# Stage 1 of a long convolution in row halves, its last quarter in two halves, the expert index spread in two row tiles, and a new order of issue

## The chip, the cores and the metric

One NeuronCore of a Trainium2 chip runs the kernel. The metric is the device time of one execution in microseconds (us), median of the runs. Engines are named as the profile names them: PE (TensorE; PEld its weight loads), DVE (VectorE), ACT (ScalarE), POOL (GpSimd), SP (SyncE, which issues nearly all DMAs).

## What is computed

Input u is [1, 2048, 512]; both halves run on the layer norm of what comes in, and each adds its result to it.

```python
# first half: a long convolution per channel (state space model, N = 128 modes)
dt = exp(log_dt); A = -exp(log_A_real) + 1j * A_imag; C = (C_real + 1j * C_imag) * dt[:, None]
P  = exp((A * dt[:, None])[:, :, None] * pos)               # 512 x 128 x 2048
K  = 2.0 * einsum("dn,dnl->dl", C, P).real                  # one filter of 2048 per channel
y  = irfft(rfft(u, 4096) * rfft(K, 4096), 4096)[:2048] + u * D_skip
# second half: 32 heads, each picks one of 16 x 16 experts
q  = einsum("nd,dhc->nhc", x, w_q); s1 = q[..., :128] @ k1.T; s2 = q[..., 128:] @ k2.T
e  = argmax(s1) * 16 + argmax(s2)                           # K = 1, so the softmax weight is 1
out = sum_h gelu(x . u[e_h]) * v[e_h]
```

## The kernel before

**Layout.** The 512 channels are worked in four quarters of 128 (c = 0 to 3). A position is l = 64 * l1 + s, with l1 of 32 and s of 64. The transform of 4096 points is done in two matmul stages, in f32, where each matmul of the code is two MATMUL instructions, each with its own LDWEIGHTS.

- *Filters* (`factors`, `tables`, `kgen`): for each of 32 table pieces i (8 to a quarter) GpSimd writes phases `pg` (L557) and magnitudes `mg` (L588, L594), ScalarE takes sine and cosine (L644 to L647), VectorE multiplies (`mg`, `gf`, L651 to L664), and a `kps` call (L690, 64 instructions on four column tiles of 32) sums over the modes. Two pieces fill one filter tile `k`, four tiles to a quarter (kt = 0 to 3).
- *Stage 1* (`stage1`, L471; `u_s1` for the signal, `k_s1` for the filter): for each tile kt two jobs of 8 matmuls. The weights are 128 x 64 (4 channels x 32 l1 in the rows, 64 values of s), the moving table `c1_s` has 128 columns (32 frequencies x 4 channels, block diagonal in the channels), real and imaginary part on two column tiles. ScalarE copies each job to `yu` or `yk` (L474).
- *Stage 2* (`stage2`, L488): 8 jobs a quarter, each 4 matmuls with full weights `c2_s` and 128 moving columns (the channels). For the signal ScalarE copies the result to `U`; for the filter (`k_s2`) VectorE multiplies it by `U` (L732, L733, L735). In the last quarter GpSimd does a third of the product (L743), out of a copy made by ScalarE (L739).
- *Inverse, first part* (`k_ia`, L764): 8 jobs a quarter, 16 instructions each, over the products. They wait for all 8 products of the quarter. ScalarE (in quarter 3 ScalarE and VectorE, L777) copies to `T`; quarters 0 to 2 go to DRAM (`t_d`), quarter 3 stays.
- *Weights of the second half* (`w_piece`): 32 pieces fold w_q with the keys (`wps`, L828), turn them (L836) and store them to DRAM (`w_d`). They are fillers; their last loads `w_q`, their high part (ScalarE) and low part `w_lo` (VectorE, L925) come at the start of the second half.
- *Second half*: 8 blocks of 256 positions. `inverse` (`ib`, L1036, then `h`, L1043), `center` and `variance` (layer norm), `scores` (`sc`, `xu`, L1150 and L1157; `index`, L1199 and L1202, gives the expert of each of 32 heads in `ix`), `select`: `ix` is transposed to `ixT` [32 heads, 256] (L1242), spread by matmuls `bc` (L1258, weights `sel` 32 x 128, one for each group of four heads) over the partitions, copied to `idxb` (L1262), compared with expert codes (`oh`, L1280), counted (`cnt`, L1290), multiplied with the gelu values, and `o` (L1327) applies v.

**Order.** Nothing is scheduled at run time. Every step is an entry of `Plan.add` (engine, a planner's price in us, the function, what it reads and writes, which PSUM buffers it takes and gives back), and a table of numbers, `ORDER`, says in which order the entries issue. Each engine executes its instructions in that order, as does SP's queue of DMAs. PSUM has seven buffers `psA` in the first half, and two `psC` and four `psD` in the second.

Of the kernel before, what the change touches and what calls it, by code (L numbers as in the profile page):

```python
# [1448 lines left out]
```

## Time and profile before

| | us |
|---|---|
| median of 3 runs | 505.17 (503.89 to 506.71) |
| profiled execution, its own time | 504.94 |
| its span, first to last instruction | 503.2 |

| engine | busy us | share of the span |
|---|---|---|
| PE | 449.0 | 89% |
| PEld | 390.3 | 78% |
| DVE | 407.8 | 81% |
| POOL | 325.5 | 65% |
| ACT | 298.3 | 59% |

The chain that ended last lies 50% on PE, 22% on DVE, and 10% each on ACT and POOL. The shares are means over the span: the table is read together with stretches of the program, as an engine can be full in one and idle in the next. The granted clock of TensorE was 0.986 of full over the run.

### The profile page before, as it was taken

The page shows a single profiled execution, that of the slowest core. Times are in us where ns is not written, and L with a number is a line of the kernel's source. Part 1 is how long each engine was busy: PE and PEld are TensorE (multiplying, and loading weights), DVE is VectorE, ACT ScalarE, POOL GpSimd, SP SyncE. Part 2 cuts the span into 40 slices and gives each one's busy share as a digit, 9 for nine tenths or more (in the row PEclk, how much of TensorE's full clock was granted, in tenths as well). Part 3 has the DMA queues.
Part 4 walks back from the last instruction along what each step waited for, and adds up shares of the span by engine and source line. Part 5 has one row for each costly group of instructions (what it writes and reads, how often), then busy time and mean ns, then how long its engine had stood idle before and what let it go on. Part 6 is the DMA issues. An engine that isn't in the chain of part 4 may idle for free.

```text
span 503.2 us, 16702 instructions
## 1 busy us (share of the span) xinstructions
PE 449.0 (89%) x7206; PEld 390.3 (78%) x7206; DVE 407.8 (81%) x708; ACT 298.3 (59%) x594; POOL 325.5 (65%) x344
## 2 busy tenths in 40 slices
PE   0266879999998999999998889999999999999985
PEld 0144568888997999889997787877878888787874
DVE  5998998899968998899745574888979686978984
ACT  4867799967987588967965362644043430416230
POOL 4989989999999999997824303572163516536130
PEclk9998799999999999999999899999999999999999
DMA  8959474234033300631017689310171311010012
GB/s 253 403 198 381 143 288 148 66 86 179 2 111 124 85 3 1 212 126 45 1 61 259 200 275 283 127 61 1 57 227 55 109 63 43 1 44 0 1 68 62
DMA packets 27362, 61.05 MB, mean 121 GB/s; under 512 B 7028, under 2 KB 14456, under 8 KB 26136
## 3 DMA queue, kind: packets, MB, share of 16 engines
q1 hardware_dynamic: 27136, 59.85, 34.9%
q8 instruction: 57, 0.93, 0.7%
q10 hardware_dynamic: 152, 0.13, 0.1%
q14 instruction: 17, 0.14, 0.1%
HBM read 46.08 MB, written 13.89 MB: 119 GB/s over the span
## 4 chain that ended last, share of the span: by engine, by line
PE 50%; DVE 22%; ACT 10%; POOL 10%; issue 4%; DMA 3%; SPq 1%; ACTq 0%; DVEq 0%; POOLq 0%
PE sc L1150 12%; PE ia L764 9%; DVE oh L1280 5%; PE s2yk L488 3%; PE xu L1157 3%; PE kps L690 3%; PE s2yu L488 3%; POOL pg L557 3%; PE s1u L471 3%; DVE st L232 2%; PE o L1327 2%; PE ib L1036 2%; PE cnt L1290 2%; ACT t L645 2%; POOL mg L594 2%
## 5 line engine op out<-in xcount | busy, mean ns | idle before, releaser
L557 POOL TENSOR_TENSOR pg<-PS 128x1024 int32<-128x1024 int32 x32 | 68.8, 2150 | 0.5
L588 POOL TENSOR_TENSOR mg<-TS 128x1024 f32<-128x1024 f32 x32 | 62.6, 1958 | 7.2 <-PE kps L690 4.5
L1280 DVE TENSOR_SCALAR oh<-idxb,ec_s 128x2048 bf16<-128x2048 bf16 (+1 forms) x72 | 50.3, 757 | 6.8 <-ACT idxb L1262 6.8
L764 PE MATMUL ia<-ca_s,U 128*128 128x128 f32 x256 | 50.6, 280 | 0.4 <-POOL U L743 0.4
L1060 POOL TENSOR_TENSOR vs<-hc 128x256 f32<-128x256 f32 x8 | 7.0, 872 | 62.6 <-ACT hc L1083 62.6
L1192 POOL TENSOR_TENSOR ks<-kq 128x512 f32<-128x512 bf16 x16 | 17.2, 1078 | 45.9 <-DVE kq L1186 44.8
L645 ACT ACTIVATE t<-t,halfpi 128x512 f32<-128x512 f32 x64 | 42.4, 662 | 2.1
L1150 PE MATMUL sc<-w_hi,hhi 128*128 128x480 f32 x128 | 42.4, 412 | 0.0
L644 ACT ACTIVATE t<-pg 128x512 f32<-128x512 int32 x64 | 38.9, 609 | 3.2 <-DVE gf L652 2.2
L764 PEld LDWEIGHTS ia<-ca_s,U 128*128 128x128 f32 x256 | 39.8, 196 | 0.6 <-POOL U L743 0.6
L647 ACT ACTIVATE t<-pg 128x512 f32<-128x512 int32 x64 | 38.2, 608 | 2.8 <-POOL pg L557 1.5
L764 PE MATMUL ia<-ca_s,yk 128*128 128x128 f32 x192 | 38.1, 280 | 0.4 <-DVE mg L664 0.4
L1150 PE MATMUL sc<-w_lo,hhi 128*128 128x480 f32 x128 | 38.4, 380 | 0.0
L1150 PE MATMUL sc<-w_hi,hlo 128*128 128x480 f32 x128 | 38.3, 380 | 0.0
L594 POOL TENSOR_TENSOR mg<-TS 128x512 f32<-128x512 f32 x32 | 37.4, 1170 | 0.4
L690 PE MATMUL kps<-mg 128*32 128x64 f32 x1024 | 34.0, 230 | 3.8 <-DVE mg L664 2.2
L488 PE MATMUL s2yk<-yk,c_s 128*128 128x128 f32 x256 | 34.7, 282 | 1.1 <-ACT yk L474 0.7
L471 PE MATMUL s1u<-c_s,xs 128*64 128x128 f32 x512 | 33.3, 277 | 2.5 <-DVE xs L508 1.6
L690 PE MATMUL kps<-gf 128*32 128x64 f32 x1024 | 33.7, 229 | 1.8 <-issue 1.8
L488 PEld LDWEIGHTS s2yk<-yk,c_s 128*128 128x128 f32 x256 | 30.6, 191 | 4.2 <-issue 1.4
L488 PE MATMUL s2yu<-yu,c_s 128*128 128x128 f32 x256 | 32.6, 279 | 0.3
L471 PEld LDWEIGHTS s1u<-c_s,xs 128*64 128x64 f32 x512 | 27.6, 137 | 5.4 <-DVE xs L508 1.7
(198 smaller groups left out, 1377.5 us busy)
## 6 DMA issues: line engine op xcount, KB each, us to landing
wq<-wq SPq DMA_DIRECT2D x25, 512.0 KB, 4.5
t_d<-T SPq DMA_DIRECT2D x24, 256.0 KB, 3.4
Tb<-t_d SPq DMA_DIRECT2D x8, 768.0 KB, 6.0
x<-xa SPq DMA_DIRECT2D x8, 512.0 KB, 5.6
xs<-xb SPq DMA_DIRECT2D x16, 256.0 KB, 5.3
xt<-xt SPq DMA_DIRECT2D x8, 512.0 KB, 4.8
out<-ob SPq DMA_DIRECT2D x7, 512.0 KB, 3.0
c_s<-wq SPq DMA_DIRECT2D x4, 512.0 KB, 8.3
```

What stands on the lines that cost most here:

```text
L471: T.matmul(ps[64 * k:64 * k + 64, g, :], lhs8(4 * n + g), c1_s[:, k], start=True, stop=True)
L488: T.matmul(ps[:, k, :], c2_s[:, kk, :], y[:, :, kk, :], start=True, stop=True)
L557: G.tensor_tensor(view(pg, 0, [[32, 2 * NC], [8, 4], [1, 8]]), view(t["PS"], 1024 + off, [[1, 2 * NC], [128, 4], [0, 8]]), view(t["PS"], 8 ...
L588: G.tensor_tensor(view(mg, 0, [[96, NC], [8, 8], [1, 8]]), view(ts, 512 + 8 * o, [[8, NC], [1, 8], [0, 8]]), view(ts, 8 * o, [[8, NC], [0, ...
L594: G.tensor_tensor(view(mg, 64, [[96, NC], [8, 4], [1, 8]]), view(ts, 1536 + o, [[1, NC], [64, 4], [0, 8]]), view(ts, 1024 + 8 * o, [[8, NC ...
L644: A.activation(p, pg[:, :, k], AF.Abs)
L645: A.activation(p, p, AF.Sin, scale=-SINSCALE, bias=halfpi)
L647: A.activation(p, pg[:, :, k], AF.Sin, scale=SINSCALE)
L690: T.matmul(kps[32 * q:32 * q + 32, 2 * g + h, :], m[:, d, 64:96], m[:, d, 0:64], start=(e == 0), stop=(e == 1))
L764: T.matmul(ps[:, g, :], t[:, 4 * n + g].rearrange("p a b -> p (a b)"), ca_s[:, s, :], start=(s == 0), stop=(s == 1))
L1150: T.matmul(ps[:, 512 * h:512 * h + 480], t[x_][:, q, ts], I[w_][:, q, 480 * h:480 * h + 480], start=(q == 0 and x_ == w_), stop=(q == 3 an ...
L1280: V.tensor_scalar(oh[:, :, 0:ln], t["idxb"][:, :, sl], S["ec"][:, 4 * e + j:4 * e + j + 1], None, op0=ALU.is_equal)
```

## The change

1. *Stage 1 in row halves* (`stage1_rows`, for u and k in quarters 2 and 3: 16 pairs of jobs). A matmul takes the upper or the lower 64 rows, which hold two of the four channels, and so 64 columns of the table (`c1_s` gets a third part of 64 columns for this). Row half h and part k give four quarters of the array; the halves write two PSUM buffers, taken together. A pair of jobs before is 32 instructions of 128 x 64 weights and 128 moving columns; now it is 64 instructions of 64 x 64 weights and 64 moving columns.
2. *Quarter 3 in halves* (`SEGS`): stage 2 of the filter, the products and `k_ia` work on 64 channels at a time. A `k_s2` job covers 8 frequencies and 64 channels in place of 4 and 128, and so has 16 instructions in place of 8. The first four `k_ia` jobs depend on the first four products, the others on the last four.
3. *Index spread in two row tiles* (`index`, `select`, `sel`): `ix` holds the 32 indices twice, `ixT` has 64 rows, `sel` is loaded twice, and a `bc` job issues the matmuls of two groups of heads in turn, on rows 0 to 31 and 32 to 63, into two `psD` buffers.
4. *A new table ORDER* of 1712 entries in place of 1728; the first 232 are as before.

```diff
+    SEGS = (1, 1, 1, 2)
...
+    HALF = dict(u=(2, 3,), k=(2, 3,))
+
+    def stage1_rows(dst, lhs8, kt, nm, r, tiles, key):
+        job, k = {}, None
+        for n in range(2):
+            def mm(n=n, job=job):
+                if n == 0:
+                    for h in range(2):
+                        bank(job, f"{nm}_{h}", h)
+                for g in range(4 * n, 4 * n + 4):
+                    for k in range(2):
+                        for h in range(2):
+                            hs = slice(64 * h, 64 * h + 64)
+                            T.matmul(flat(job[h], 64)[64 * k:64 * k + 64, g], lhs8(g)[hs], c1_s[hs, k, 128:192],
+                                     start=True, stop=True)
+
+            k = plan.add("PE", 0.56, mm, r=r, t=tiles, take=() if n else ("psA", "psA"), after=[k] if n else [], n_mm=32)
+        for h in range(2):
+            def ev(h=h, job=job):
+                A.copy(dst()[:, 8 * kt:8 * kt + 8, :, 2 * h:2 * h + 2],
+                       flat(job[h], 64).rearrange("p g (k d) -> p g k d", d=2))
+
+            plan.add("ACT", 0.54, ev, w=[key + (kt, h)], t=tiles, give="psA", after=[k])
+
     def stage1(dst, lhs8, kt, nm, r, tiles, key):
+        if key[1] in HALF[key[0][1]]:
+            return stage1_rows(dst, lhs8, kt, nm, r, tiles, key)
...
     def k_s2(c):
...
+            sg, nk = k4 * ns // 8, 4 * ns
+            g_, k_ = slice(32 * sg // ns, 32 * (sg + 1) // ns), slice(nk * (k4 % (8 // ns)), nk * (k4 % (8 // ns)) + nk)
+            kts = range(4 * sg // ns, 4 * (sg + 1) // ns)
+            deps = [("yk", c, kt, n) for kt in kts for n in range(2)]
...
+            def mm(job=job, g_=g_, k_=k_, k4=k4, nk=nk):
+                ps = flat(bank(job, f"s2yk{c}_{k4}"), 512 // nk)
+                for kk in range(k_.start, k_.stop):
+                    T.matmul(ps[:, kk - k_.start, :], c2_s[:, kk, :], spectrum(c, "yk")[:, g_, kk, :], start=True, stop=True)
...
+            k = plan.add("PE", 0.98 if ns == 1 else 1.15, mm, r=deps + u_k + ["c2"], t=tiles, take="psA", n_mm=8 * ns)
...
     def k_ia(c):
         plan.group = f"ia{c}"
-        deps = [("P", c, k4) for k4 in range(8)]
         for n in range(8):
-            job = {}
+            job, sg = {}, n * SEGS[c] // 8
+            deps = [("P", c, k4) for k4 in range(8 * sg // SEGS[c], 8 * (sg + 1) // SEGS[c])]
...
-            for g in range(0, 8, hj):
+            for g in range(0, 8, 2 * hj):
                 job = {}
 
                 def mm(job=job, g=g, sl=sl, ln=ln, hj=hj):
-                    job["ps"] = bp = I["psD"].tile([P, hj, ln], F32, tag="m", name=f"bc{b}_{g}_{ln}")
+                    for r in range(2):
+                        job[r] = I["psD"].tile([P, hj, ln], F32, tag="m", name=f"bc{b}_{g}_{ln}_{r}")
                     for h in range(hj):
-                        T.matmul(bp[:, h], S["sel"][:, g + h, :], t["ixT"][:, sl], start=True, stop=True)
+                        for r in range(2):
+                            rs = slice(32 * r, 32 * r + 32)
+                            T.matmul(job[r][:, h], S["sel"][rs, g + hj * r + h, :], t["ixT"][rs, sl], start=True, stop=True)
...
-                n = plan.add("PE", 0.23, mm, r=[("ixT", p), "sel"], t=[kX, kB], take="psD", n_mm=hj)
+                n = plan.add("PE", 0.27, mm, r=[("ixT", p), "sel"], t=[kX, kB], take=("psD", "psD"), n_mm=2 * hj)
```

**What moves: PE around the last table piece.** In each row stand the line, the instruction, out <- in, and the shape; `x8` counts repeats. `s1k_2_1` is stage 1 of the filter, tile 2, job 1 (now: row half 1); `s2yu_7` is job 7 of stage 2 of the signal; `wps` and `wpt` belong to a piece of w. All are of quarter 3. Before:

```order
L828 MATMUL wps_3899<-wq_3886,ka_s 32x128 x4
L828 MATMUL wps_3899<-wq_3886,kb_s 32x128 x4
L836 MATMUL wpt_3910<-ident,wt_3897 128x128
L836 MATMUL wpt_3913<-ident,wt_3908 128x128
L471 MATMUL s1k_0_1_3917<-c_s,k_0_3380 64x128 x8
L471 MATMUL s1k_0_0_3930<-c_s,k_0_3380 64x128 x8
L471 MATMUL s1k_1_1_3939<-c_s,k_1_3649 64x128 x8
L471 MATMUL s1k_2_1_3959<-c_s,k_2_3840 64x128 x8
L690 MATMUL kps_3_3853<-mg_3828 32x64 x4
L690 MATMUL kps_3_3853<-gf_3849 32x64 x4
```

Now, behind the same `kps` calls:

```order
L476 MATMUL s1k_0_0_4239<-c_s,k_0_3656 64x64
L476 MATMUL s1k_0_1_4240<-c_s,k_0_3656 64x64
L514 MATMUL s2yu_7_4276<-yu_2892,c_s 128x128 x4
L514 MATMUL s2yu_6_4283<-yu_2892,c_s 128x128 x4
L476 MATMUL s1k_2_0_4288<-c_s,k_2_4107 64x64
L476 MATMUL s1k_2_1_4289<-c_s,k_2_4107 64x64
```

Four stage-1 jobs of the filter and two pieces of w stood directly ahead of the last `kps` rows, and the last four pieces of w behind them. Now all pieces of w are issued earlier, and the four stage-1 pairs of the filter stand behind those rows, with the last two `s2yu` jobs among them.

**PE at the end of the first half.** `s2yk_0` to `s2yk_7` are stage 2 of the filter, `ia` the inverse's first part. Before:

```order
L488 MATMUL s2yk_0_4050<-yk_3952,c_s 128x128 x4
L488 MATMUL s2yk_1_4060<-yk_3952,c_s 128x128 x4
L488 MATMUL s2yk_2_4072<-yk_3952,c_s 128x128 x4
L488 MATMUL s2yk_3_4079<-yk_3952,c_s 128x128 x4
L828 MATMUL wps_4089<-wq_4070,ka_s 32x128 x4
L828 MATMUL wps_4089<-wq_4070,kb_s 32x128 x4
L488 MATMUL s2yk_4_4103<-yk_3952,c_s 128x128 x4
L836 MATMUL wpt_4108<-ident,wt_4101 128x128
L828 MATMUL wps_4114<-wq_4112,ka_s 32x128 x4
L828 MATMUL wps_4114<-wq_4112,kb_s 32x128 x4
L488 MATMUL s2yk_5_4123<-yk_3952,c_s 128x128 x4
```

Now:

```order
L476 MATMUL s1k_3_0_4351<-c_s,k_3_4348 64x64
L476 MATMUL s1k_3_1_4352<-c_s,k_3_4348 64x64
L757 MATMUL s2yk_2_4394<-yk_4236,c_s 128x64 x8
L757 MATMUL s2yk_3_4417<-yk_4236,c_s 128x64 x8
L757 MATMUL s2yk_4_4456<-yk_4236,c_s 128x64 x8
L757 MATMUL s2yk_7_4465<-yk_4236,c_s 128x64 x8
L757 MATMUL s2yk_5_4474<-yk_4236,c_s 128x64 x8
L757 MATMUL s2yk_6_4483<-yk_4236,c_s 128x64 x8
L803 MATMUL ia_0_4498<-ca_s,yu_2892 128x128
L803 MATMUL ia_0_4498<-ca_s,U_3705 128x128
```

The pieces of w between the `s2yk` jobs are gone, the jobs have twice the instructions at half the columns, and two of them (0 and 1) stand among the stage-1 rows above this piece. `ia` follows directly.

**DVE at the start of the second half.** `T` are the copies of `ia3`. Before:

```order
L777 COPY T_4229<-ia_6_4281 64x64x4 x2
L777 COPY T_4229<-ia_2_4319 64x64x4 x2
L777 COPY T_4229<-ia_4_4337 64x64x4 x2
L925 TENSOR_TENSOR w_lo<-w_q_4309,w_hi 128x960
L925 TENSOR_TENSOR w_lo<-w_q_4312,w_hi 128x960
L1043 TENSOR_TENSOR h_4418<-ib_0_4366,xt_4316 128x4x128
L1043 TENSOR_TENSOR h_4418<-ib_1_4383,xt_4316 128x4x128
L1073 TENSOR_TENSOR hc_4463<-h_4418,mean_0_4458 128x4x128
```

Now:

```order
L986 CAST ident_b<-ident 128x128
L987 MEMSET ones_d 128x128
L964 TENSOR_TENSOR w_lo<-w_q_4441,w_hi 128x960
L816 COPY T_4525<-ia_4_4599 64x64x4 x2
L816 COPY T_4525<-ia_5_4590 64x64x4 x2
L816 COPY T_4525<-ia_6_4608 64x64x4 x2
L816 COPY T_4525<-ia_7_4627 64x64x4 x2
L1017 CAST sel_s<-sel_f 64x1024
L1082 TENSOR_TENSOR h_4709<-ib_0_4659,xt_4554 128x4x128
L1082 TENSOR_TENSOR h_4709<-ib_1_4676,xt_4554 128x4x128
```

The last `w_lo` pieces stand ahead of the last copies of T, and the cast of `sel` between these copies and the first `h`.

## Rows read from the trace of the kernel before

**Rows 1.** Stretches: us, busy us of each engine (instructions), granted clock, DMA share, GB/s

```profile
0.00:75.00 75.00, 39.40 (x830) 28.86 (x832) 65.62 (x176) 55.31 (x140) 62.85 (x72) 0.93 0.78 279
75.00:262.07 187.07, 183.00 (x3437) 168.98 (x3433) 160.66 (x264) 152.20 (x294) 170.31 (x156) 1.00 0.25 82
262.07:281.84 19.77, 16.24 (x265) 14.06 (x263) 11.83 (x20) 10.77 (x24) 10.11 (x8) 1.00 0.67 229
281.84:297.73 15.89, 15.89 (x126) 15.77 (x127) 8.45 (x19) 9.00 (x18) 0.00 (x0) 0.89 0.91 291
...
307.10:458.04 150.94, 150.01 (x1820) 125.45 (x1820) 118.77 (x164) 52.82 (x87) 72.09 (x96) 1.00 0.24 81
```

**Rows 2.** What POOL waited for, 75 to 256 us: total us, times, longest

```profile
POOL mg L588 <- PE kps L690: 4.5, 3, 2.8
...
POOL mg L588 <- issue: 1.1, 1, 1.1
```

**Rows 3.** Timeline of POOL, end of first half: start, us, engine, line, operation, [idle before]

```profile
254.08 1.16 POOL L594 TENSOR_TENSOR mg<-TS 128x512 f32<-128x512 f32 x1
270.08 1.27 POOL L743 TENSOR_TENSOR U<-ki,U 64x512 f32<-64x512 f32 x1 [14.84 <-DVE yu L732]
...
280.53 1.26 POOL L743 TENSOR_TENSOR U<-ki,U 64x512 f32<-64x512 f32 x1 [0.18 <-DVE yu L732]
```

**Rows 4.** Timeline of PE, 262 to 298 us

```profile
262.07 0.32 PE L690 MATMUL kps<-mg 128*32 128x64 f32 x8
...
272.66 0.43 PE L828 MATMUL wps<-wq,ka_s 128*32 128x128 f32 x8 [1.32 <-DMA wq<-wq]
...
273.24 1.16 PE L488 MATMUL s2yk<-yk,c_s 128*128 128x128 f32 x8
...
281.84 0.71 PE L764 MATMUL ia<-ca_s,U 128*128 128x128 f32 x2 [0.36 <-POOL U L743]
...
285.58 0.39 PE L764 MATMUL ia<-ca_s,yu 128*128 128x128 f32 x2
...
297.41 0.39 PE L764 MATMUL ia<-ca_s,U 128*128 128x128 f32 x2
```

**Rows 5.** Chain of work that ended last: start, us, engine, tile, line, instructions

```profile
144.54 1.90 PE s1k L471 x32
...
170.29 0.89 PE s2yk L488 x8
171.19 1.03 PE kps L690 x64
...
213.92 0.89 PE kps L690 x64
```

**Rows 6.** Groups by line: busy us, mean ns of one, idle us before them

```profile
L664 DVE TENSOR_TENSOR mg<-mg,t 128x512 f32<-128x512 f32 x32 | 21.9, 684 | 5.6 <-ACT t L645 4.6
...
L474 ACT COPY yk<-s1k 128x512 f32<-128x512 f32 x32 | 17.9, 596 | 0.7 <-PE s1k L471 0.6
...
L1258 PE MATMUL bc<-ixT,sel_s 32*128 32x256 bf16 (+1 forms) x72 | 10.1, 258 | 0.0
...
L242 PEld LDWEIGHTS mu<-st,eq 128*128 128x128 f32 x4 | 0.5, 190 | 0.6 <-ACT t L645 0.6
```

**Rows 7.** Timeline around the mean of the layer norm, 59 us

```profile
59.36 0.52 PEld L242 LDWEIGHTS mu<-st,eq 128*128 128x128 f32 x4 [0.60 <-ACT t L645]
59.39 0.68 PE L242 MATMUL mu<-st,eq 128*128 128x64 f32 x4 [0.39 <-DVE st L232]
```

**Rows 8.** Timeline of DVE, start of the second half

```profile
299.51 2.23 DVE L925 TENSOR_TENSOR w_lo<-w_q,w_hi 128x960 fp32r<-128x960 f32 x2
301.77 1.29 DVE L1043 TENSOR_TENSOR h<-ib,xt 128x512 f32<-128x512 f32 x2
...
307.76 0.67 DVE L978 CAST sel_s<-sel_f 32x1024 bf16<-32x1024 f32 x1
```

**Rows 9.** Timeline of PE, an index spread

```profile
347.25 0.82 PE L1258 MATMUL bc<-ixT,sel_s 32*128 32x256 bf16 x6
```

More of the change, by code (lines that the diff above doesn't have):

```diff
@@ L194 @@
     eq8t = wk.tile([P, 32], F32, name="eq8t")
-    c1_s = wk.tile([P, 2, 128], F32, name="c1_s")
+    c1_s = wk.tile([P, 2, 192], F32, name="c1_s")
     c2_s = wk.tile([P, 32, 128], F32, name="c2_s")
@@ L470, in mm @@
                     for k in range(2):
-                        T.matmul(ps[64 * k:64 * k + 64, g, :], lhs8(4 * n + g), c1_s[:, k], start=True, stop=True)
+                        T.matmul(ps[64 * k:64 * k + 64, g, :], lhs8(4 * n + g), c1_s[:, k, 0:128], start=True, stop=True)
             def ev(n=n, job=job):
@@ L717, in k_s2, with views, prod @@
         plan.group = f"k2{c}"
-        deps = [("yk", c, kt, n) for kt in range(4) for n in range(2)]
+        ns = SEGS[c]
         tiles = [f"yk{c}", f"yu{c}" if c > 2 else f"yk{c}", f"U{c}"]
-        u_k = [("U", c, k) for k in range(8)] if c > 2 else []
         for k4 in range(8):
-            job, k = stage2(c, "yk", k4, deps + u_k + [("U", c, k4)], tiles)
-            def prod(job=job, k4=k4):
-                U, yk = Q[c]["U"], Q[c]["yk" if c < 3 else "yu"]
-                if c < 3:
-                    pv = job["ps"].rearrange("p k (g d) -> p g k d", d=4)
-                    uv, kv = (t[:, :, 4 * k4:4 * k4 + 4] for t in (U, yk))
-                else:
-                    pv = job["ps"].rearrange("p k m -> p m k")
-                    uv, kv = (four(c, t, k4).rearrange("p g d k -> p (g d) k") for t in (U, yk))
+            sg, nk = k4 * ns // 8, 4 * ns
+            g_, k_ = slice(32 * sg // ns, 32 * (sg + 1) // ns), slice(nk * (k4 % (8 // ns)), nk * (k4 % (8 // ns)) + nk)
+            kts = range(4 * sg // ns, 4 * (sg + 1) // ns)
+            deps = [("yk", c, kt, n) for kt in kts for n in range(2)]
+            u_k = [("U", c, k) for k in range(8)] if c > 2 else [("U", c, k) for k in range(k_.start // 4, k_.stop // 4)]
+            job = {}
+            def mm(job=job, g_=g_, k_=k_, k4=k4, nk=nk):
+                ps = flat(bank(job, f"s2yk{c}_{k4}"), 512 // nk)
+                for kk in range(k_.start, k_.stop):
+                    T.matmul(ps[:, kk - k_.start, :], c2_s[:, kk, :], spectrum(c, "yk")[:, g_, kk, :], start=True, stop=True)
+            def views(job=job, g_=g_, k_=k_, nk=nk):
+                ps = flat(job["ps"], 512 // nk)
+                U, yk = Q[c]["U"], spectrum(c, "yk" if c < 3 else "yu")
+                if c < 3:
+                    return [ps.rearrange("p k (g d) -> p g k d", d=4)] + [t[:, g_, k_] for t in (U, yk)]
+                return [ps.rearrange("p k m -> p m k")] + [
+                    t.rearrange("p g k d -> p g (k d)").rearrange("p g (d k) -> p g d k", d=4)[:, g_, :, k_].rearrange(
+                        "p g d k -> p (g d) k") for t in (U, yk)]
+            def prod(views=views):
+                pv, uv, kv = views()
                 V.tensor_mul(kv, pv, uv)
@@ L735, in prod, with part, rest @@
                     V.tensor_mul(uv[0:64], pv[64:128], uv[0:64])
-            def part(job=job, k4=k4):
-                job["ki"] = wk.tile([P, 128, 4], F32, tag="kt", name=f"ki{k4}", bufs=3)
-                A.copy(job["ki"][0:64], job["ps"].rearrange("p k m -> p m k")[64:128])
-            def rest(job=job, k4=k4):
-                uv = four(c, Q[c]["U"], k4).rearrange("p g d k -> p (g d) k")
+            def part(job=job, k4=k4, nk=nk):
+                job["ki"] = wk.tile([P, 512 // nk, nk], F32, tag="kt", name=f"ki{k4}", bufs=3)
+                A.copy(job["ki"][0:64], flat(job["ps"], 512 // nk).rearrange("p k m -> p m k")[64:128])
+            def rest(job=job, views=views):
+                pv, uv, kv = views()
                 G.tensor_tensor(uv[0:64], job["ki"][0:64], uv[0:64], op=ALU.mult)
+            k = plan.add("PE", 0.98 if ns == 1 else 1.15, mm, r=deps + u_k + ["c2"], t=tiles, take="psA", n_mm=8 * ns)
             if c < 3:
-                plan.add("DVE", 2.14, prod, r=[("U", c, k4)], w=[("P", c, k4)], t=tiles, give="psA", after=[k])
+                plan.add("DVE", 2.14, prod, r=u_k, w=[("P", c, k4)], t=tiles, give="psA", after=[k])
             else:
@@ L750, in k_s2 @@
                 a = plan.add("ACT", 0.52, part, w=[ki], t=[ki], after=[k])
-                v = plan.add("DVE", 1.43, prod, r=[("U", c, k4)], t=tiles, give="psA", after=[k, a])
+                v = plan.add("DVE", 1.43, prod, r=u_k, t=tiles, give="psA", after=[k, a])
                 plan.add("POOL", 1.5, rest, r=[ki], w=[("P", c, k4)], t=[ki, f"U{c}"], after=[v])
@@ L957, in open_peer @@
         I["wp"] = ctx.enter_context(tc.tile_pool(name="wp", bufs=1, side="right", reuse_waits="tile"))
-        S["sel"] = I["wp"].tile([32, 8, 128], BF16, name="sel_s")
+        S["sel"] = I["wp"].tile([64, 8, 128], BF16, name="sel_s")
         I["psC"] = ctx.enter_context(tc.tile_pool(name="psC", bufs=2, space=PSUM, reuse_waits="tile"))
@@ L1200, in index @@
             ef = ei.rearrange("p (h a) -> p h a", a=2)
-            t[f"ix{k}"] = hp_("ix", n, [P, 32], BF16)
-            V.scalar_tensor_tensor(t[f"ix{k}"], ef[:, :, 0], 16.0, ef[:, :, 1], op0=ALU.mult, op1=ALU.add)
+            t[f"ix{k}"] = hp_("ix", n, [P, 64], BF16)
+            a, b_ = (ef[:, :, j].unsqueeze(1).to_broadcast([P, 2, 32]) for j in range(2))
+            V.scalar_tensor_tensor(t[f"ix{k}"].rearrange("p (c h) -> p c h", c=2), a, 16.0, b_, op0=ALU.mult, op1=ALU.add)
         def gelu():
@@ L1239, in mm @@
             def mm(job=job, ks_=ks_, lo=lo):
-                job["ps"] = tp = I["psD"].tile([32, 256], BF16, tag="m", name=f"ixt{b}_{lo}")
+                job["ps"] = tp = I["psD"].tile([64, 256], BF16, tag="m", name=f"ixt{b}_{lo}")
                 for k in ks_:
@@ L1251, in select, with ev @@
             hj = 512 // ln
-            for g in range(0, 8, hj):
+            for g in range(0, 8, 2 * hj):
                 job = {}
                 def mm(job=job, g=g, sl=sl, ln=ln, hj=hj):
-                    job["ps"] = bp = I["psD"].tile([P, hj, ln], F32, tag="m", name=f"bc{b}_{g}_{ln}")
+                    for r in range(2):
+                        job[r] = I["psD"].tile([P, hj, ln], F32, tag="m", name=f"bc{b}_{g}_{ln}_{r}")
                     for h in range(hj):
-                        T.matmul(bp[:, h], S["sel"][:, g + h, :], t["ixT"][:, sl], start=True, stop=True)
-                def ev(job=job, g=g, sl=sl, hj=hj):
-                    idxb = tile_of(t, "idxb", lambda: hp_("idxb", b, [P, 8, 256], BF16))
-                    A.copy(idxb[:, g:g + hj, sl], job["ps"])
-                n = plan.add("PE", 0.23, mm, r=[("ixT", p), "sel"], t=[kX, kB], take="psD", n_mm=hj)
-                plan.add("ACT", 0.50, ev, w=[("idxb", p, g)], t=[kB], give="psD", after=[n])
+                        for r in range(2):
+                            rs = slice(32 * r, 32 * r + 32)
+                            T.matmul(job[r][:, h], S["sel"][rs, g + hj * r + h, :], t["ixT"][rs, sl], start=True, stop=True)
+                n = plan.add("PE", 0.27, mm, r=[("ixT", p), "sel"], t=[kX, kB], take=("psD", "psD"), n_mm=2 * hj)
+                for r in range(2):
+                    def ev(job=job, g=g, sl=sl, hj=hj, r=r):
+                        idxb = tile_of(t, "idxb", lambda: hp_("idxb", b, [P, 8, 256], BF16))
+                        A.copy(idxb[:, g + hj * r:g + hj * r + hj, sl], job[r])
+                    plan.add("ACT", 0.50, ev, w=[("idxb", p, g + hj * r)], t=[kB], give="psD", after=[n])
             idx_k = [("idxb", p, g) for g in range(0, 8, hj)]
@@ L1359, in _constants @@
     a = two * np.outer(l1, k1 + 0.5) / 64
-    c1 = np.zeros((4, 32, 2, 32, 4))
+    c1 = np.zeros((4, 32, 2, 192))
     for q in range(4):
-        c1[q, :, 0, :, q] = np.cos(a)
-        c1[q, :, 1, :, q] = -np.sin(a)
+        for p, v in ((0, np.cos(a)), (1, -np.sin(a))):
+            c1[q, :, p, 0:128].reshape(32, 32, 4)[:, :, q] = v
+            c1[q, :, p, 128:192] = np.stack([v * (q % 2 == d) for d in range(2)], -1).reshape(32, 64)
     ang = two * ((k1[:, None, None] + 0.5) * s[None, :, None] / 4096 + s[None, :, None] * k2[None, None, :] / 64)
@@ L1396, in _constants @@
     f = np.float32
-    return s, dict(c1=c1.reshape(128, 256).astype(f), c2=c2.reshape(128, 4096).astype(f),
+    return s, dict(c1=c1.reshape(128, 384).astype(f), c2=c2.reshape(128, 4096).astype(f),
                    ca=ca.reshape(128, 256).astype(f), cb=cb.reshape(128, 64, 64).astype(f),
                    keys=keys.astype(f), ecode=ecode.astype(f), hsel=hsel.astype(f),
-                   sel=sel.reshape(32, 8, 128).astype(f))
+                   sel=np.concatenate([sel.reshape(32, 8, 128)] * 2).astype(f))
 _INS = ["xa", "xb", "xt", "lar", "aim", "cre", "cim", "ldt", "dsk", "wq", "ka", "kb", "ue", "ve",
```

4 lines of the change are left out of this document (2 added, 2 removed), and 143 rows, old and new, of the table ORDER.

## The prediction

> **What bounds the kernel now.** Read the stretches first [rows 1]. From 75 to 262 us TensorE is busy 183.0 of 187.1 us and GpSimd 170.3, so the convolution has two full engines at once. Which of them a shorter step helps is told by GpSimd's waits [rows 2]: over 75 to 256 us it waits 4.5 us for `kps` matmuls and 1.1 us for nothing seen; nothing else there holds it for long. It is therefore nearly a bound of its own: its last table piece ends at 254.08 + 1.16 = 255.24 us [rows 3] and, without these 5.6 us, could not end before 249.6.
>
> Next the end of the convolution [rows 4]. The last `kps` call starts at 262.07. Then `s2yk` jobs alternate with `wps` pieces that wait for a load (1.32 us), and `ia3` waits until GpSimd has finished the last product: 280.53 + 1.26 = 281.79 [rows 3]. Its first matmul pair then lasts 0.71 us, one from 285.58 on 0.39: the granted clock of the stretch is 0.89, so this is the 1.2 GHz level after a stretch in which TensorE was busy only 16.24 of 19.77 us. `ia3` ends at 297.41 + 0.39 = 297.80. From 307 to 458 us TensorE is busy 150.0 of 150.9 us [rows 1]: there what TensorE saves is saved.
>
> **Stage 1 in row halves.** 16 pairs of jobs change (u and k of quarters 2 and 3, four tiles each). A pair before is 32 instructions in 1.90 us [rows 5]. Afterwards it is 64 instructions of 64 rows and 64 columns with 64 moving columns, on four quarters of the array in turn. The trace has no row-tiled matmul. Its nearest row is a `kps` call: also 64 instructions with 64 moving columns, on four column tiles, 0.89 us when it follows its like and 1.03 after a change of shape [rows 5]. I take 1.03, a saving of 0.87 us a pair. The other end is that only the two column tiles run side by side, as before: 32 instructions of 128 moving columns took 1.90, so 64 of half the columns take 1.90 again, a saving of nothing.
>
> The Trainium skill, "TensorE: Matmul & The Clock Gate", section on LDWEIGHTS, says that a weight load takes as long as its columns, not its rows, so a half-height load costs a whole one; that speaks against this part and would give 64 x 53 ns = 3.4 us a pair (an estimate from that page) if loads stood in line. The trace agrees only in part: `kps` issues 64 loads in 0.89 us, 14 ns each, against a page price of 27 ns for 32 columns, so loads to different column tiles overlap; row tiles are shown by no row here. The Trainium skill, "TensorEngine Tiling (Array Packing)", section Tiling Modes, has the tiles load and multiply in parallel, which would leave 1.03.
>
> Each pair still has two ScalarE copies of 128x512, now into a strided view. A copy there costs 596 ns [rows 6]; if the view made each a tenth dearer, 32 copies would add 1.9 us to an engine with 35 us to spare from 75 to 262 us [rows 1]. I add nothing; without that spare time the 1.9 would count.
>
> **The last quarter in halves.** A `s2yk` job of quarter 3 goes from 8 instructions with 128 moving columns to 16 with 64, all with full 128x128 weights. The row that has just this shape is `mu`: four full loads, each with 64 moving columns, start 0.11 us apart (0.52 us for the four, 0.19 for one [rows 6]: 0.33 over three steps; the four matmuls take 0.68) [rows 7]. A job of 8 takes 0.89 [rows 5], also 0.11 each. So halving the columns halves nothing: 16 x 0.11 = 1.76 us, plus 0.87 a job, 8 jobs, **plus 7.0 us** on TensorE. The other end is the price in the diff's planner, 1.15. In return `ia3`'s first four jobs need only the first four products. The products on GpSimd, each behind its two on VectorE, come every 1.5 us now (270.08 to 280.53, seven steps [rows 3]), faster than the new jobs, so when the eighth job is done only the last one or two products are open, and `ia3` starts at once with the first half (7 us of work). The wait before `ia3` and the slow clock in it should go.
>
> **The order, up to the last `kps` call.** TensorE has less in front of that call: 12 of the 16 pairs at 0.87 (10.4 us); four jobs of k-stage-1 that stood ahead (3.8) and two `s2yu` jobs (1.8) now stand behind it. Four `wps` pieces come ahead, about 0.7 each (2.8; 272.66 to 273.24 for the matmuls, then a transpose [rows 4]). Their four loads and two stores move on SP's queue ahead of the store of T of quarter 2; what waits for that store, the first T loads of the second half, is wanted 30 us later, so I cost this at nothing. Net 13.2: 262.07 - 13.2 = 248.9. GpSimd's bound is 249.6 and about 1 us for the last VectorE product (0.68 [rows 6]) and its hand-over, so 250.6. Two engines that are both full cannot both run without a gap; I take 252, **minus 10.1 us**. The ends are 250.6 and 262 (the table chain finds other waits, on ScalarE or VectorE, busy 152 and 161 of 187 us).
>
> **From that call to the end of `ia3`.** Before: 297.80 - 262.07 = 35.7 us. After: `kps` 1.03, four pairs 4.1, two `s2yu` 1.8, eight `s2yk` 14.1, `ia3` 128 matmuls at (297.41 - 285.58)/106 = 0.112, so 14.3; with some 0.6 for changes of shape 36.0. **Plus 0.3**: what the wait, the clock and the four pieces give back, the doubled weight loads eat. Ends: minus 5 (at 1.15 a job) and plus 2.
>
> **Start of the second half.** Two `w_lo` pieces, 2.23 us, stand between the last copy of T and the first `h` [rows 8], and the first `mean` waits for that `h`. In the new order they stand ahead of the last copies; the cast of `sel` (0.67) comes in their place. **Minus 1.6.** The w_q loads behind them are issued earlier, as the w pieces are done before the tables are. If a load were late, four copies of T would queue behind that `w_lo`: up to plus 2.
>
> **Index spread.** Six `bc` matmuls take 0.82 us [rows 9] and one alone about 0.26 [rows 6], so 0.11 each behind the first; eight to a block. Two side by side save 0.44 a block, over 7 blocks where TensorE is full 3.1. Against it a job now needs two of the four psD buffers at once. I take **minus 2.5**; ends 0 and minus 3.5. The index instruction writes 64 columns, not 32, on a VectorE with some 30 us to spare there [rows 1]: nothing.
>
> **Loads.** The table for stage 1 grows by 64 KB; at 279 GB/s, the rate of the first 75 us [rows 1], that is **plus 0.2**. The other moves of the order in the second half I cost at nothing: TensorE has only 0.9 us idle to win from 307 to 458 us, and the tail behind it, where it is VectorE's turn in part, I give 2 to 3 us either way.
>
> **Sum.** -10.1 + 0.3 - 1.6 - 2.5 + 0.2 = -13.7. The profiled execution took 504.94 us, so 491.2; the median of the runs, 505.17, lies 0.2 above it. Forecast **491.5 us**.
>
> **Rivals.**
> Row halves do not run side by side. Against it stands only the likeness to `kps`. The 16 pairs then cost 1.90 as before. Up to the last `kps` call only the moves count, -2.8; I take -2. Behind it four pairs cost 3.5 more, +3.8. The index spread gains nothing. -2 + 3.8 - 1.6 + 0.2: about **505.3**, no change.
> Slower: the loads of the halves stand in line. A load of 128 columns starts every 0.11 us [rows 7], so one of 64 columns may every 0.055, and a pair takes 64 x 0.055 = 3.5 us, 1.6 more than now: 16 x 1.6 = 26 on TensorE, which is full. With the +0.4 of the case before, about **531**. This case decides from about 2.05 us a pair: 1.03 and (13.7 + 2.5)/16. For it: no row shows row tiles. Against it: `kps` and the old stage 1 both overlap their loads. The Trainium skill, "TensorE: Matmul & The Clock Gate", section on LDWEIGHTS, is this case if nothing overlaps.
> The table chain does not shorten by much. GpSimd, VectorE and ScalarE are all over 80% busy there [rows 1], and GpSimd's order is changed too (pieces of the next tables drawn ahead). If only its 4.5 us of `kps` waits are half won, -3 in place of -10: about **498.5**.
> The halves of `s2yk` cost what the planner says, 1.15: -4.9 more, **486.5**. `mu` speaks against it.
>
> **How the numbers follow.** Forecast 0.68 (487 to 496 with the ends of its terms), table chain 0.11, cheap halves 0.06, no overlap of row halves 0.09, loads in line 0.06. The range of 8 in 10 takes the first three and leaves out the last two and a little below: 484 to 503. A measurement can tell 0.5%, 2.5 us, from no change. Faster by more than that: the first three, less a little of the second, 0.83. Same: most of the fourth, 0.08. Slower: the last and the rest of the fourth, 0.09.
>
> **What would show it.** A 64x64 stage-1 pair at 1.0 to 1.1 us in TensorE's rows (1.9: the rival). `s2yk` of quarter 3 at 16 instructions in 1.76 us (1.15: cheap halves). The last `kps` call at 251 to 254 us, with GpSimd's `mg` waits for `kps` near nothing. No wait before `ia3` and no pair of it near 0.71 us. `h` of block 0 directly behind the copies of T. A `bc` job of four matmuls holding TensorE for about 0.25 us. The forecast is wrong if the last `kps` call stands after 257 us or `ia3` ends after 293.

## The result, and the profile after

The changed kernel takes 507.86 us (median of 20 runs, 506.27 to 509.41), the kernel before 505.34 (20 runs, 502.43 to 509.0): ratio **1.0049, 95% interval 1.0029 to 1.0068**. That is no gain, but a small loss of 0.3 to 0.7%; forecast were 491.5 us and a range that ends at 503. All medians here are over every run, while the ratios leave out runs that were over 1.5% above the fastest of their kernel (two of six in e1, one of six in e10). The profiled executions have spans of 503.2 and 507.2 us. By their marks:

| stretch, us | before | forecast | after |
|---|---|---|---|
| up to the start of the last `kps` call | 262.07 | 252 | 265.15 |
| from there to the end of `ia3` | 35.7 | 36.0 | 37.9 |
| from there to the end of the span | 205.4 | 201.3 | 204.1 |

First what came as forecast, or near it. TensorE's groups by line and shape, of the changed kernel:

```profile
L476 PE MATMUL s1k<-c_s,k 64*64 64x64 f32 x512 | 11.2, 233 | 4.2 <-DVE k L728 1.4 <-issue 1.1 <-DVE mg L686 0.8
L476 PE MATMUL s1u<-c_s,xs 64*64 64x64 f32 x512 | 10.9, 228 | 0.5 <-DVE mg L686 0.5
...
L757 PE MATMUL s2yk<-yk,c_s 128*128 128x64 f32 x128 | 14.9, 276 | 0.0
...
L1301 PE MATMUL bc<-ixT,sel_s 32*128 32x256 bf16 x56 | 5.1, 272 | 0.0
L1301 PE MATMUL bc<-ixT,sel_s 32*128 32x128 bf16 x16 | 1.0, 215 | 0.1
```

The row halves do run side by side: 1024 matmuls, 16 pairs, in 22.1 us, 1.38 a pair where a pair of whole rows took 1.90 [rows 5] and 1.03 was forecast. The spread takes 6.1 us where it took 10.1 [rows 6]. TensorE's timeline behind the last `kps` call:

```profile
265.15 0.32 PE L716 MATMUL kps<-mg 128*32 128x64 f32 x8
...
266.18 1.73 PE L476 MATMUL s1k<-c_s,k 64*64 64x64 f32 x98
269.00 0.69 PE L476 MATMUL s1k<-c_s,k 64*64 64x64 f32 x30 [1.09 <-issue]
...
277.82 10.93 PE L757 MATMUL s2yk<-yk,c_s 128*128 128x64 f32 x96
288.59 0.44 PE L803 MATMUL ia<-ca_s,yu 128*128 128x128 f32 x2
289.09 0.39 PE L803 MATMUL ia<-ca_s,yu 128*128 128x128 f32 x2
```

Six `s2yk` half jobs take 10.86 us, 1.81 each, and `ia` follows with no wait and no pair near 0.71 us [rows 4 has both]. What failed shows in the stretches (columns as in [rows 1]) and in GpSimd's waits from 75 to 265 us:

```profile
75.00:265.22 190.22, 179.19 (x3832) 162.04 (x3824) 161.14 (x264) 153.28 (x296) 171.00 (x156) 0.98 0.29 94
265.22:288.75 23.53, 22.44 (x465) 21.69 (x466) 10.23 (x16) 12.40 (x21) 6.62 (x6) 1.00 0.66 222
288.75:303.11 14.36, 14.36 (x132) 14.24 (x133) 12.44 (x23) 8.15 (x18) 3.50 (x3) 1.00 0.60 183
...
200.00:225.00 25.00, 21.08 (x667) 18.43 (x665) 16.31 (x26) 19.20 (x38) 20.26 (x18) 0.86 0.35 117
```

```profile
POOL mg L614 <- PE kps L716: 12.0, 4, 5.0
POOL mg L614 <- DVE gf L681: 2.3, 1, 2.3
```

TensorE had 3.8 us less to do in front of that call than before (179.19 against 183.00 us), but was idle for 11.0 us where it had been for 4.1, and part of its work ran at a lower clock: 0.86 granted from 200 to 225 us. GpSimd's wait for `kps` did not go; it rose from 4.5 us [rows 2] to 12.0.

The chain of waits through that stretch (start, us, engine, tile, line) tells where TensorE stood:

```profile
204.77 1.19 PE s1k L476 x62
...
205.99 1.21 ACT yk L482 x2
207.20 0.49 ACT t L673
...
208.41 0.66 ACT t L671
209.07 0.51 ACT k L724
...
210.80 0.69 DVE mg L690
211.49 0.60 DVE mg L685
212.09 0.61 DVE mg L686
...
212.74 1.88 PE s1k L476 x59
...
216.59 2.02 PE s2yk L757 x8
```

A stage-1 job waits for tile `k`, whose copy stands on ScalarE behind evictions and sines. The next waits for VectorE's `mg` products. It reads no `mg`; what it waits for is a PSUM bank that a table's cosine still holds. TensorE's timeline has these gaps:

```profile
209.90 1.21 PE L476 MATMUL s1k<-c_s,k 64*64 64x64 f32 x64 [1.43 <-DVE k L728]
211.54 0.39 PE L476 MATMUL s1k<-c_s,k 64*64 64x64 f32 x2 [0.43 <-DVE mg L690]
212.74 1.88 PE L476 MATMUL s1k<-c_s,k 64*64 64x64 f32 x59 [0.81 <-DVE mg L686]
```

Behind them (1.43, 0.43 and 0.81 us from 208.5 to 212.7) 59 matmuls take 1.88 us where 62 took 1.19, and a `s2yk` job 2.02 where it takes 0.89 [rows 5]: the 1.2 GHz level (granted 0.50 from 214 to 218 us, 1.00 again from 218.5 us on).

### The profile page after: what moved, and what is told of

The parts are those of the page before. It is cut to its first block, busy times and chain, and to the rows that moved or that the text cites. A ratio compares the mean times of both kernels' runs of the same rounds, so it can differ in the third digit from the quotient of the medians.

```text
span 507.2 us, 17851 instructions
## 1 busy us (share of the span) xinstructions
PE 446.7 (88%) x7782; PEld 386.3 (76%) x7782; DVE 411.4 (81%) x708; ACT 301.4 (59%) x596; POOL 327.5 (65%) x344
## 4 chain that ended last, share of the span: by engine, by line
PE 57%; DVE 23%; ACT 8%; POOL 5%; issue 4%; DMA 2%; SPq 0%; DVEq 0%; POOLq 0%; ACTq 0%
PE sc L1189 14%; PE ia L803 10%; PE s2yk L757 6%; PE o L1371 4%; DVE oh L1324 3%; PE kps L716 3%; PE cnt L1334 3%; PE s2yu L514 3%; PE ib L1075 3%; PE xu L1196 2%; DVE st L232 2%; DVE U L773 2%; POOL pg L583 2%; PE s1k L476 2%; DVE yk L770 2%
## 5 line engine op out<-in xcount | busy, mean ns | idle before, releaser
L1324 DVE TENSOR_SCALAR oh<-idxb,ec_s 128x2048 bf16<-128x2048 bf16 (+1 forms) x72 | 51.4, 763 | 6.3 <-ACT idxb L1307 6.2
L1231 POOL TENSOR_TENSOR ks<-kq 128x512 f32<-128x512 bf16 x16 | 18.6, 1162 | 47.2 <-DVE kq L1225 47.2
L757 PE MATMUL s2yk<-yk,c_s 128*128 128x128 f32 (+1 forms) x320 | 42.6, 285 | 1.7 <-DVE U L773 0.9
L757 PEld LDWEIGHTS s2yk<-yk,c_s 128*128 128x128 f32 x320 | 38.4, 195 | 4.5 <-issue 1.1
L803 PEld LDWEIGHTS ia<-ca_s,yk 128*128 128x128 f32 x192 | 29.0, 191 | 4.7 <-DVE mg L690 1.9
L1099 POOL TENSOR_TENSOR vs<-hc 128x256 f32<-128x256 f32 x8 | 5.9, 736 | 41.1 <-ACT hc L1122 41.1
L1233 POOL TENSOR_TENSOR ks<-ks 128x256 f32<-128x256 f32 (+2 forms) x48 | 29.9, 624 | 3.8
```

Source lines behind the costliest of these rows:

```text
L757: T.matmul(ps[:, kk - k_.start, :], c2_s[:, kk, :], spectrum(c, "yk")[:, g_, kk, :], start=True, stop=True)
L803: T.matmul(ps[:, g, :], t[:, 4 * n + g].rearrange("p a b -> p (a b)"), ca_s[:, s, :], start=(s == 0), stop=(s == 1))
L1324: V.tensor_scalar(oh[:, :, 0:ln], t["idxb"][:, :, sl], S["ec"][:, 4 * e + j:4 * e + j + 1], None, op0=ALU.is_equal)
```

## Experiments

Each kernel was timed beside the kernel before on its own chip, so ratios are compared, not times. "Order of before" and "new order" are the two lists that set the order of issue.

**Operations and order apart.** e1 to e4 change only which operations are on and which list orders them.

e1, all three operations, order of before.

> All three operations of the change, issued in the order of the kernel before (an eviction moves back only where its second matmul job now has to come first). Theory A (the operations are worth what they were priced at; the new order loses it, because between 204 and 240 us it leaves TensorE waiting on one chain and puts the kps calls behind stage 1 and stage 2, so that GpSimd waits for its two mg buffers): 494 to 500 us, from 505.3, -10 for the 16 pairs at up to 0.64 us each before the last kps call, -2.5 to -4 for the index spread, +7 to +8 for s2yk. Theory B (the row halves themselves do it in any order: a pair takes two PSUM banks at once, and both evictions wait for both jobs): 504 to 510 us.

Measured: 527.72 us, ratio 1.0436 (1.0408 to 1.0463).

e2, no operation, new order.

> None of the three operations, all in the new order (jobs of the last quarter's stage 2 and inverse that would need halves moved behind what they read). Theory A: the order alone costs, so slower than the changed kernel by what the operations save, 511 to 520 us. Theory B: the order is harmless, 503 to 506 us.

Measured: 516.91 us, 1.0260 (1.0241 to 1.0279). **The order alone costs 2.6%, about 13 us**: the last `kps` call starts at 264.12, `ia3` ends at 309.0, the second half takes 208.0 us. Its TensorE timeline has the price of the largest piece:

```profile
290.46 0.80 PE L765 MATMUL ia<-ca_s,yu 128*128 128x128 f32 x2 [7.38 <-DVE yu L733]
```

e3, row halves alone, order of before (the index spread in one row tile, as in e8, and):

```diff
-    SEGS = (1, 1, 1, 2)
+    SEGS = (1, 1, 1, 1)
```

> Row halves in stage 1 of quarters 2 and 3 alone, in the order of the kernel before. Theory A: 494 to 500 us (16 pairs at 0.5 to 0.64 us, less what GpSimd's tables don't follow). Theory B: 504 to 510 us, with TensorE waits at the row-half jobs.

Measured: 519.91 us, 1.0292 (1.0268 to 1.0315). In that order the two jobs of a pair can stand far apart, and both banks are held between them. TensorE's timeline, the first pair of u in quarter 2:

```profile
125.58 0.69 PE L478 MATMUL s1u<-c_s,xs 64*64 64x64 f32 x32
...
142.13 0.32 PE L718 MATMUL kps<-mg 128*32 128x64 f32 x8 [2.07 <-DVE mg L688]
...
151.83 0.69 PE L478 MATMUL s1u<-c_s,xs 64*64 64x64 f32 x32
```

Two of seven banks are gone for 26 us, and a `kps` call waits 2.07 us for one: the product that the row names is of a later table, whose last product ran until 142.60 us, when the call had already started. So neither A nor B as I put them: the new order is bad for the old operations, the old order worse for the new ones.

e4, index spread alone, order of before (`HALF` empty, `SEGS` all 1).

> Index spread in two row tiles alone, in the order of the kernel before. The forecast's term: 502.8 us (-2.5); by the 4.0 us that line 1301 saved in busy time, at most -4: 501.3 us. If the second half waits on ScalarE or VectorE and not on TensorE: 505 us, no change.

Measured: 506.95 us, 1.0067 (1.0037 to 1.0096): slower, though line 1302 took 6.4 us in place of 10.1. Its profile has `ia3` end at 296.1 and a second half of 209.5 us, 4.1 more than before; what costs these was not tried.

**Banks or matmuls.** e5 keeps e3's order and its two banks a pair, with the matmuls of whole rows:

```diff
-                        for h in range(2):
-                            hs = slice(64 * h, 64 * h + 64)
-                            T.matmul(flat(job[h], 64)[64 * k:64 * k + 64, g], lhs8(g)[hs], c1_s[hs, k, 128:192],
-                                     start=True, stop=True)
+                        T.matmul(job[n][64 * k:64 * k + 64, g, :], lhs8(4 * n + g), c1_s[:, k, 0:128], start=True, stop=True)
```

> The order of e3 and its way with PSUM (stage 1 of quarters 2 and 3 takes both banks ahead of the first job, and both are evicted behind the second job), but the matmuls of the kernel before, 128x64 and whole rows. Theory B (what made e3 slow is that a pair holds two of the seven banks, and lets them go late): no faster than e3's 519.9 us, 516 to 528 us, since the matmuls themselves are 0.6 us a pair slower. Theory C (the row-half matmuls or their evictions themselves made e3 slow, the banks don't matter): 504 to 508 us, as before.

Measured: 510.53 us, 1.0145 (1.0117 to 1.0172): between the two. Holding both banks of a pair, and copying them late, costs 7 us without any row half; here the second bank is first written by the second job, which e3 does by the first. That this is the other half of e3's loss was not tried apart.

**One operation undone, in the new order.** e6: whole rows.

```diff
-    HALF = dict(u=(2, 3,), k=(2, 3,))
+    HALF = dict(u=(), k=())
```

> The changed kernel with stage 1 in whole rows again (one bank a job), the last quarter's halves, the index spread and the new order kept. If the row halves give what they were priced at (16 pairs, 0.64 us each): 515 to 518 us. If their gain is lost again to waits for banks and to the slow clock of 213 to 220 us: 504 to 508 us, no slower than the changed kernel.

e7: the last quarter whole (`SEGS` all 1).

> The changed kernel with the last quarter of stage 2 whole again (SEGS all 1; the jobs that needed halves stand behind what they read). In e2 the first inverse jobs of the last quarter waited 7.4 us for the products and TensorE fell to 0.80 of its clock; the halves cost 7.9 us more in line 757. If the halves pay for themselves by that wait: 505 to 511 us. If the wait (7.4 us and what the slow clock adds) was worth more than they cost: 512 to 518 us.

e8: the spread in one row tile.

> The changed kernel with the index spread in one row tile again. By the busy time of its line, 4.0 us less with row tiles: 511 to 512 us. If, as in e4, the two banks that a pair takes cost more than that: 503 to 507 us.

Measured: e6 509.43 us, 1.0128 (1.0105 to 1.0151); e7 515.06, 1.0251 (1.0223 to 1.0280); e8 508.60, 1.0112 (1.0090 to 1.0135). Against the changed kernel's 1.0049 the row halves are worth 0.8% (4 us), the last quarter's halves 2.0% (10 us), the spread 0.6% (3 us). They don't add up: e7, with row halves and spread, is as slow as e2 with none. And the row halves do nothing for the last `kps` call: it starts at 263.91 us in e6, at 265.15 with them.

**GpSimd's wait as the cause.** e9 moves only pieces of the last ten tables.

> The changed kernel; of its order only pieces of the last ten tables move (TensorE: the kps calls of tables 30 and 31 five jobs later, behind inverse jobs that are ready; ScalarE: sines of tables 26 and 27 three to six jobs earlier; VectorE: two products of table 24 three jobs later; GpSimd: pieces of tables 24 and 28 moved within their neighbours). Theory D (the operations are worth their price; the new order's queues of 204 to 265 us lose it, head of line): the waits of GpSimd for kps (12.0 us) shrink, last kps call by 262 us or before, 500 to 505 us. If the operations lose it wherever the tables stand: 507 to 509 us.

Measured: 505.38 us, 1.0039 (1.0021 to 1.0057), no different from the change. GpSimd's wait for `kps` fell from 12.0 to 7.0 us; the last `kps` row is no earlier (266.73, after 265.95). To cut that wait by 5.0 us won no time here: it is a sign more than the cause.

**Other orders.** From here to e16 each kernel has a list of its own; e12 has the last quarter whole, e15 whole rows, e11 and e16 none of the three operations.

> The three operations in a third order, made for them with the prices that the trace shows (a half job of s2yk 1.81 us; seven PSUM banks, free again in the order in which they are let go). Theory D: 484 to 496 us, last kps call about 256, last inverse job of quarter 3 by 290 us. Theory B (the operations lose in any order): 502 us or more.

> The operations of the kernel before in an order made for them in the same way as that of e10. Theory D: the order alone is worth 3 to 10 us, 495 to 502 us, and e10 stands 8 to 13 us below this one: that difference is what the operations are worth when each set has its own order. Theory B: this one is as fast as e10 or faster.

> Row halves and index spread, the last quarter's stage 2 whole, in an order made for them in the same way. The halves of the last quarter let the inverse start at once (e7: 7.4 us of wait without them) but cost 7.9 us in line 757: if these cancel, within 2 us of e10; if the early start is worth more, 4 to 10 us slower than e10.

Measured: e10 509.66 us, 1.0119 (1.0075 to 1.0163); e11 526.57, 1.0440 (1.0401 to 1.0479); e12 519.05, 1.0303 (1.0276 to 1.0329). They say little on the convolution, since their second halves were put in another order too and took 214 to 221 us. In e10 `ia3` ends at 298.1, 5 us before the changed kernel's, with the last `kps` call at 270.5: an early last call is not what makes an early end. So e13 to e16 leave the second half alone.

> All three operations; the order of the second half is the changed kernel's, only the convolution's jobs are put in another order, in which TensorE's queue waits less (made with traced prices, the half job of s2yk at 1.81 us). Theory D (the order loses the gain): last kps call by 260, last inverse job by 296 us, 494 to 501 us. Theory E (GpSimd's tables keep the last kps call at 262 to 266 us in any order, and 37 us of work stand behind it): 503 to 508 us.

> As e13, another order made from e9's, with more room against late pieces. Theory D: 495 to 502 us. Theory E: 503 to 508 us. If e13 and e14 differ by more than 4 us, orders made from prices can't be told apart by them.

> As e13, with stage 1 in whole rows and an order made for that. If the row halves are worth something once the order suits them: 4 to 8 us slower than e13. If TensorE's saving in stage 1 goes into waits in any order: within 2 us of e13.

> The operations of the kernel before, convolution in another order made in the same way, second half as before. Theory D: the order of before was already good for its operations, 500 to 506 us, and e13 is 4 to 10 us faster than this one. If any order made so gains the same: this one is as fast as e13.

Measured: e13 520.74 us, 1.0327 (1.0297 to 1.0358; more on it at the end); e14 505.26, 1.0018 (0.9989 to 1.0048); e15 504.63, 1.0016 (0.9992 to 1.0040); e16 511.40, 1.0134 (1.0091 to 1.0177). By what was set down for them e13 and e14 differ too much to compare single orders. What stands is that no order tried beats the kernel before, and that with an order of its own each, whole rows (e15) and row halves (e14) come out alike. The lists differ by more than the operations do: beside a list made in the same way for none of them, all three are 3.1% ahead in e10 (against e11) and 1.2% in e14 (against e16), but 1.9% behind in e13; and e11 and e16, the operations of before in such lists, are 4.4% and 1.3% slower than in the list they had.

e17 takes e14's list with whole rows.

> The order of e14 to the letter, stage 1 in whole rows. If what the row halves save on TensorE (e14 against e15: 177.9 and 184.6 us busy from 75 to 262 us) is worth time in an order that suits them: 509 to 513 us, 4 to 8 us above e14. If it only makes TensorE wait elsewhere: 503 to 507 us, as e14.

Measured: 510.03 us, 1.0128 (1.0099 to 1.0157). In one and the same order, made for them, the row halves are worth 1.1%, 5.5 us. The stretch from 75 to 262 us, one line from each of the profiles of e14, e15 and e17:

```profile
75.00:262.00 187.00, 177.85 (x3877) 162.65 (x3879) 158.35 (x260) 152.77 (x297) 168.94 (x153) 1.00 0.30 97
```

```profile
75.00:262.00 187.00, 184.57 (x3483) 169.71 (x3484) 159.43 (x262) 152.22 (x297) 170.17 (x153) 1.00 0.29 93
```

```profile
75.00:262.00 187.00, 183.79 (x3435) 168.45 (x3432) 158.23 (x260) 151.11 (x296) 168.36 (x153) 1.00 0.29 97
```

With whole rows TensorE is full (184.57 of 187); with row halves it has 6.7 us less to do and stands idle for them.

e18 asks whether its idle time comes with the number of instructions:

```diff
-                        T.matmul(ps[64 * k:64 * k + 64, g, :], lhs8(4 * n + g), c1_s[:, k, 0:128], start=True, stop=True)
+                        for cs in ((slice(0, 64), slice(64, 128)) if key[1] > 1 else (slice(0, 128),)):
+                            T.matmul(ps[64 * k:64 * k + 64, g, cs], lhs8(4 * n + g), c1_s[:, k, cs], start=True, stop=True)
```

> The order of e15, whole rows, but each stage-1 matmul of quarters 2 and 3 in two, with 64 moving columns each: as many instructions as the row halves, no row tile, one bank a job. Theory F (the gaps in which TensorE waits for nothing seen, 5.9 us in e14 and 0.9 in e15 from 75 to 310 us, come with the number of instructions in those stretches): such gaps appear here too, 2 to 6 us from 75 to 310 us. Theory G (they come from row tiles): at most 1.8 us. A pair then takes 1.9 us if the matmuls bound it, 64 x 0.055 = 3.5 us if the loads do; the time 505 to 530 us accordingly.

Measured: 507.90 us, 1.0082 (1.0053 to 1.0110). TensorE's waits for nothing seen, 75 to 310 us, in e14 and then in e18:

```profile
PE kps L717 <- issue: 3.7, 5, 1.2
...
PE s1k L477 <- issue: 2.2, 1, 2.2
```

```profile
PE kps L718 <- issue: 1.1, 1, 1.1
...
PE wps L869 <- issue: 0.4, 1, 0.4
```

1.5 us against 5.9: the number of instructions does not bring them, F falls. A pair takes 2.2 us here, about 1.2 in e14, so the rate of instructions may; no run here tests it, and what the traces say of it stands at the end.

## Why the prediction was wrong, step by step

**The step that failed is "up to the last `kps` call": minus 10.1, measured plus 3.1.** It holds 13.2 us of the forecast's error; the profiles differ by plus 4.0 (the medians by 2.5) where minus 13.7 was foreseen. The step took 13.2 us of work off TensorE and gave 3.1 of them back as idle time, 248.9 to 252. The stretch from the span's start to that call, in the kernel before, the changed kernel and e6 (the same order, whole rows):

```profile
0.00:262.07 262.07, 222.40 (x4261) 197.84 (x4261) 226.28 (x438) 207.51 (x433) 233.16 (x227) 0.98 0.40 138
```

```profile
0.00:265.15 265.15, 217.98 (x4633) 190.07 (x4633) 226.20 (x438) 208.01 (x435) 232.75 (x227) 0.97 0.43 146
```

```profile
0.00:263.91 263.91, 223.63 (x4249) 196.58 (x4249) 226.37 (x438) 207.54 (x435) 232.74 (x227) 0.99 0.42 146
```

Work fell by 4.4 us (222.40 to 217.98), 8.8 less than foreseen; idle time rose by 7.5 (39.67 to 47.17), 4.4 more than foreseen. So two thirds of the miss are work that stayed, one third is waiting. It went wrong in three ways.

- It took 10.4 us off TensorE for the row halves and let the call come earlier by that, bounded only by GpSimd. By e6 they take off 5.7 us (223.63 to 217.98): a pair costs 1.19 us at full clock (19.0 us for 16 in e14), not 1.03, and 1.38 in the changed kernel, part of it at 1.2 GHz. And not even that reached the call, since idle time rose by 6.9 us with them (40.28 to 47.17). The queue waited for ScalarE's copies and VectorE's products in the order in which they stand, and for banks. I had written "the table chain finds other waits, on ScalarE or VectorE" as the far end of this term, 262, and gave the rival 0.11; it was the case, and beyond that end.
- It priced the moved instructions by their duration alone, -2.8. In e6 they add 1.2 us of work in place of that (222.40 to 223.63): by their rows the four pieces of w come to 4.0 us, not 2.8, the four stage-1 jobs take 2.4 away, not 3.8, and the same `ia` matmuls take 1.6 more (47.3 against 45.7). e2 shows the new order to cost 13 us by itself, 2.05 of them before this call, most of the rest as the wait of 7.38 us in front of `ia3`, with the clock at 0.89 from 264.2 to 309.0 us. I read which rows changed place on TensorE, but not what each then waits for.
- It counted psD's two buffers for the spread as a cost but not the two psA banks that a row-half pair takes before its first matmul and gives back behind its second job. e3 and e5 show that holding them costs in the order of before; in the new order the waits for banks at 211.5 and 212.7 us are what is seen of it.

**From that call to the end of `ia3`: plus 0.3, measured plus 2.2.** The parts were near: half jobs at 1.81 us (forecast 1.76), at the pitch of full loads that the row of `mu` had, no wait and no slow clock before `ia3`. The rest is a gap of 1.09 us in stage 1 and pairs that are dearer than 1.03. Against the kernel before the two sides nearly cancel, as forecast; in the new order the halves are worth 10 us, since without them `ia3` waits (e7, e2).

**Second half: minus 4.1, measured minus 1.3.** The first `h` stands 3.2 us behind the end of `ia3` (306.29), 4.0 before: half of the 1.6. It is not directly behind the cast, but waits 0.79 us for `ib`. The spread's busy time fell by 4.0 us, more than the 2.5 of the forecast; e8 puts its worth at 0.6%, 3 us. What takes it back shows in part: TensorE's waits for the index `ix` rose from 0.4 to 2.7 us, and 1.7 of them are there in e8 too, so they come with the order.

**Loads in line**, the slower rival at 3.5 us a pair, fell: a pair took 1.19 us at full clock, 18.6 ns for each of its 64 loads, so loads to the four tiles overlap. The Trainium skill, "TensorE: Matmul & The Clock Gate", section on LDWEIGHTS, taken without overlap gave 3.4 us a pair (an estimate from that page). "TensorEngine Tiling (Array Packing)" in the Trainium skill, section Tiling Modes, says that different tiles load and multiply in parallel; here the trace agrees with that page.

That the time came out near the 505.3 us of the rival without overlap is chance: the row halves do overlap, and a small loss with row halves that overlap was no case of the prediction.

What stays open: whether TensorE's pauses where row halves run are waits for its instructions, as the traces suggest (last section), and whether an order exists in which the three operations win. No kernel run here showed one.

## What to carry to other kernels

A saving on a full engine is worth what its neighbours can follow: before counting it, walk its queue in the new order and name for each job the copy, product or PSUM bank that it waits for, then the clock after such a gap. An operation that takes its buffers earlier and gives them back later has to be priced with them, and with the order that it was made for; here the same row halves were worth nothing, 4 us or minus 15 us, by the order. Compare the engine's work up to each mark too, not only its waits: two thirds of what failed to come here were work. Test order and operation apart, both ways round.
